# All q and k transposed by PE, the whole residual by transposing transfers, single PSUM banks and a new list: retention followed by a gated MLP

## Chip, core and metric

The kernel runs on one core of a Trainium2 chip. The core has five engines that run on their own queues: PE (TensorE, matmuls, with its weight loads shown apart as PEld), DVE (VectorE), ACT (ScalarE), POOL (GpSimd) and SP (SyncE, which here only issues transfers). They meet through semaphores. [...] Sixteen DMA engines carry the transfers. The metric is the device time of one execution in microseconds (us), lower is better.

## What is computed

Eight sequences of 576 positions, eight heads of 64. The first part is a retention layer: scores without softmax, each multiplied by a power of the head's decay, and zero for keys behind the query. The second is a gated MLP whose gate mixes positions with a 576 x 576 matrix.

```python
scores = scale * np.matmul(q, k.transpose(0, 1, 3, 2))
Dmat = np.where(rel >= 0, gamma[:, None, None] ** rel[None, :, :], 0.0)
x = heads_side_by_side(np.matmul(scores * Dmat, v))      # (8, 576, 512)
h = gelu_tanh(x @ w_in)                                  # (8, 576, 1024)
u, v = h[..., :512], h[..., 512:]
v_n = (v - mean(v)) / np.sqrt(var(v) + 1e-06) * g_ln
v_s = np.einsum('ts,bsd->btd', w_sg, v_n) + b_sg[None, :, None]
out = x + (u * v_s) @ w_out
```

## The kernel before

**Tiling.** Two sequences make a pair p (0 to 3): 1152 positions, nine tiles of 128. Tile 4 holds the end of one sequence and the start of the other. Each pair is cut into five blocks (`RB`): four of 256 positions and, in the middle, one of 128. Blocks are numbered b = 0 to 19. The decay is split into a power for the query and one for the key or value, so that only the block's own part needs a mask (0 or 1), and what lies before a block comes from a running state.

**Steps of a block.** `a_load` loads q, k, v (lines 324 and 327; q of two neighbouring blocks at once, tile `ldq`, except in the joint blocks 0, 1 and the middle ones, which keep q and k in one tile and are transposed together). `a_prep` (lines 340 to 370) multiplies q and v by the powers and casts k to bf16, mostly on POOL. Then q and k are transposed so that the head's dimension lies on partitions: by PE in `a_T` (line 407: 32 matmuls with an identity for a unit of 2048 columns) and a copy from PSUM on DVE, `a_Tev` (line 422), or by one transposing transfer, `a_TX` (line 427). Two limits, `TBQ` and `TBK`, both 10, say up to which block PE does it: pairs 0 and 1 by PE, and in pairs 2 and 3 all but the joint blocks by transfers. `a_S` (line 458) computes the scores of two heads' pairs at a time, `a_Sev` (lines 471, 474) multiplies them by the mask on DVE. `a_Z` (line 494) computes k^T v, `a_Zsum` and `a_Zev` (lines 519 to 528) keep the running state in fp32 and a bf16 copy. `a_O` and `a_O2` (line 540) sum the block's own part and the state's part, `a_Oev` (line 597) moves the result to the tile `xT` on ACT.

**Steps of the MLP.** For each tile i: `m_V` (line 608), gelu on ACT (`m_Vg`, line 615), mean and variance on DVE (`m_stats`, lines 623 and 624), the factor on POOL (`m_rs`, lines 628 to 631), normalizing on ACT (`m_norm`, lines 640 and 643). `m_U` (line 655) and `m_Ug` (line 665) give u in transposed form. `m_W` (line 674) mixes the positions of a sequence with the transposed w_sg (`wT`, built by PE at line 792), `m_Wg` (line 684) multiplies by u on DVE. `m_O` (line 705) multiplies by w_out. The residual x is added in one of two ways: for pairs below `XP` (= 1, so pair 0) by four identity matmuls into the same PSUM tile (line 700) and a plain copy on ACT (line 722), for the others by a transposing transfer `m_X` (line 716) and an add on DVE (line 724). `m_store` (line 729) stores 128 rows.

**PSUM.** Two pools: `psP` has two tiles of two banks each (transposes, scores, outputs of a block), `psD` four tiles of one bank (all else). A tile that is asked for waits until the reader of the tile that held its place is done.

**Order.** All steps are jobs with a number, and `ORDER` (lines 20 to 54) is a list of job numbers written out: it is the order in which the steps are issued, and so the order of each engine's queue. `f2w128` and the like are filler matmuls on a tile of zeros (line 225). `3@267` holds job 3, a load on SP's queue, until PE has done job 267; eleven transfers are held so. The planner class emits the list and does not reorder it. The durations and due times given to `add` are not used when the kernel is built.

Of the kernel before, what the change touches and what calls it, by code (L numbers as in the profile page):

```python
# [61 lines left out]
class Job:  # L62
    def __init__(self, eng, dur, due, fn, deps=(), new=None, uses=(), mode=None, nbytes=0, run=0, what="", behind=None, since=0.0, lag=0.0, ins=0, port=False, parts=1):
# [12 lines left out]
class Planner:  # L76
# [27 lines left out]
def kernel(  # L104
# [46 lines left out]
    XP = 1  # L151
    TBQ, TBK = 10, 10
# [65 lines left out]
    def fill(spec):  # L218
# [3 lines left out]
        def f():  # L222
            scr = psD.tile([128, 512], F32, name="scr", tag="d")
# [18 lines left out]
    def win_load(half):  # L242
# [22 lines left out]
    def sg_load():  # L265
# [821 lines left out]
```

## Time and profile before

| what | us |
|---|---|
| time, median of 3 runs | 209.55 |
| lowest and highest run | 209.48, 209.73 |
| span of the profiled execution, first to last instruction | 207.8 |
| ACT busy, evictions of x (line 597) | 20.8 |
| ACT busy, normalizing (line 643) | 25.2 |
| DVE busy, gate products (line 684) | 27.6 |
| DVE busy, statistics (line 623) | 24.6 |
| POOL waiting for DVE's statistics (line 628) | 36.5 |

The profile is one execution, of which only the span is given: the time that the runs measure includes what lies before the first and behind the last instruction. Busy time counts an engine's instructions as the profiler recorded them. The ends of matmuls are modelled, so for a row of them the distance from one start to the next tells what they cost. In a line of the groups, `DVE COPY qT<-pp 128x2048 bf16<-128x2048 bf16 x5 | 6.1, 1214 | 2.1` reads: five copies, 6.1 us together, 1214 ns each, and 2.1 us of idle time on the engine just before them. An arrow in brackets names what ended that idle time.

### The profile page before, as it was taken

How to read it: one execution, taken by the hardware profiler on the slowest of the kernel's cores; microseconds unless marked ns; L12 is line 12 of the kernel's file. 1: busy time of each engine (PE TensorE's matmuls, PEld its weight loads, DVE VectorE, ACT ScalarE, POOL GpSimd, SP SyncE). 2: the span in 40 equal slices, each digit the busy share in tenths (PEclk: the TensorE clock that was granted, in tenths of full speed). 3: DMA queues.
4: the chain of work that ended last, by engine and by line, in shares of the span. 5: the costliest groups of instructions: out<-in, count | busy, mean ns of one | idle time of the engine just before them, and what ended most of it. 6: DMA issues, size and time to landing. Idle time of an engine off the chain costs nothing. (4 is left out here: it accounts for less than half of the span.)

```text
span 207.8 us, 7603 instructions
## 1 busy us (share of the span) xinstructions
PE 189.1 (91%) x3231; PEld 130.0 (63%) x3260; DVE 146.6 (71%) x287; ACT 116.3 (56%) x207; POOL 118.3 (57%) x169
## 2 busy tenths in 40 slices
PE   3277989999999979999999999999999999999992
PEld 3256467786667655666777676676675776556651
DVE  3767549897597669646968479669695648876672
ACT  5263398864659436689477565745827580536300
POOL 8747348864858799884659628760558813022000
PEclk9999999999999999999999999999999999999998
DMA  5999989989958999599999989999899999659765
GB/s 163 287 313 215 312 282 317 295 241 326 304 123 226 264 335 336 161 231 174 221 288 351 179 183 333 250 139 206 232 299 334 182 242 253 171 169 169 261 140 203
DMA packets 93844, 50.45 MB, mean 243 GB/s; under 512 B 44970, under 2 KB 87218, under 8 KB 93810
## 3 DMA queue, kind: packets, MB, share of 16 engines
q1 hardware_dynamic: 93792, 49.96, 93.8%
q8 instruction: 25, 0.41, 0.9%
q14 instruction: 9, 0.07, 0.1%
q10 hardware_dynamic: 18, 0.00, 0.0%
HBM read 32.79 MB, written 9.44 MB: 203 GB/s over the span
## 5 line engine op out<-in xcount | busy, mean ns | idle before, releaser
L471 DVE TENSOR_TENSOR ret<-pp,msk 128x1024 bf16<-128x1024 f32 x32 | 38.3, 1214 | 7.5 <-PE pp L458 7.4
L674 PE MATMUL wp<-wT,vn 128*128 128x288 bf16 x256 | 40.6, 286 | 0.0
L370 POOL TENSOR_TENSOR vb<-ld,gpow 128x1024 bf16<-128x1024 f32 (+1 forms) x20 | 34.5, 1731 | 10.2 <-PE pp L458 6.1
L608 PE MATMUL hv<-w_in,xT 128*128 128x512 bf16 x132 | 36.5, 393 | 1.9 <-ACT xT L597 1.0
L684 DVE TENSOR_TENSOR uT<-wp,uT 128x288 bf16<-128x288 f32 x64 | 27.6, 450 | 14.9 <-PE wp L674 10.3
L655 PE MATMUL hu<-xT,w_in 128*128 128x256 bf16 (+1 forms) x320 | 36.3, 262 | 0.0
L615 ACT ACTIVATE vg<-hv 128x512 f32<-128x512 f32 x36 | 21.2, 595 | 25.0 <-PE hv L608 20.7
L705 PE MATMUL op<-w_out,uT 128*128 128x512 bf16 (+1 forms) x131 | 33.5, 373 | 0.8 <-issue 0.2
L655 PEld LDWEIGHTS <-w_in 128*128 128x128 bf16 x320 | 28.1, 98 | 6.2
L623 DVE BATCH_NORM_STATS2 bst<-vg 128x6 f32<-128x512 f32 x36 | 24.6, 683 | 8.8 <-ACT vg L615 8.7
L597 ACT ACTIVATE xT<-pp 128x512 bf16<-128x512 f32 (+1 forms) x40 | 20.8, 549 | 17.2 <-PE pp L540 17.2
L370 POOL TENSOR_TENSOR qb<-ldq,gpow 128x1024 bf16<-128x1024 f32 x14 | 26.4, 1902 | 5.3 <-DMA ldq<-in_q_dram 5.3
L674 PEld LDWEIGHTS <-vn 128*128 128x128 bf16 x256 | 24.3, 98 | 8.2
L643 ACT ACTIVATE vn<-vg,mv 128x512 bf16<-128x512 f32 x32 | 25.2, 809 | 6.5 <-POOL mv L631 6.4
L628 POOL TENSOR_SCALAR mv<-mv 128x2 f32<-128x2 f32 (+1 forms) x20 | 4.5, 224 | 41.6 <-DVE mv L624 36.5
L665 ACT ACTIVATE uT<-hu 128x512 bf16<-128x512 f32 x36 | 20.7, 594 | 10.2 <-PE hu L655 10.1
L724 DVE TENSOR_TENSOR ob<-op,xr 128x512 f32<-128x512 f32 (+1 forms) x28 | 18.4, 669 | 5.8 <-PE op L705 5.5
L608 PEld LDWEIGHTS <-xT 128*128 128x128 bf16 x144 | 13.4, 100 | 14.2 <-ACT xT L597 1.6
L705 PEld LDWEIGHTS <-uT 128*128 128x128 bf16 x148 | 13.5, 98 | 11.4
L674 PE MATMUL wp<-wT,vmid 128*128 128x288 bf16 x64 | 18.2, 287 | 0.1
L360 POOL CAST kb<-ld 128x1024 bf16<-128x1024 f32 x14 | 14.5, 1037 | 4.8 <-DMA ld<-in_k_dram 4.8
L629 POOL TENSOR_TENSOR mv<-mv,mhalf 128x2 f32<-128x2 f32 (+1 forms) x20 | 14.1, 705 | 1.7
(100 smaller groups left out, 238.2 us busy)
## 6 DMA issues: line engine op xcount, KB each, us to landing
out_dram<-ob SPq DMA_DIRECT2D x35, 256.0 KB, 3.1
ld<-in_v_dram SPq DMA_DIRECT2D x16, 512.0 KB, 5.7
ld<-in_k_dram SPq DMA_DIRECT2D x16, 512.0 KB, 6.5
ldq<-in_q_dram SPq DMA_DIRECT2D x7, 1024.0 KB, 10.4
xT<-in_moe_w_sg_dram SPq DMA_DIRECT2D x2, 576.0 KB
ld<-in_q_dram SPq DMA_DIRECT2D x2, 512.0 KB, 5.2
xT<-in_moe_w_in_dram SPq DMA_DIRECT2D x1, 1024.0 KB
ld<-in_q_dram SPq DMA_DIRECT2D x8, 128.0 KB, 4.2
```

Source lines behind the costliest of these rows:

```text
L370: ve.tensor_tensor(dst, src, g.unsqueeze(len(src.shape) - 1).to_broadcast(list(src.shape)), op=Alu.mult)
L471: ins = nc.vector.tensor_tensor(ret[:].rearrange("p r (k t) -> p (r k) t", k=2), sc[:].rearrange("p r (k t) -> p (r k) t", k=2), (msk2 if ...
L597: nc.scalar.activation(dst, src, Act.Copy)
L608: ins = nc.tensor.matmul(hv[:], xTs[p][:, m, kk, :], w_in[:, kk, F2:], start=(kk == 0), stop=(kk == KK - 1))
L615: unfence(nc.scalar.activation(vgs[i][:], cur.pop(("hv", i))[:], Act.Gelu_apprx_tanh), ("V", i))
L623: nc.vector.bn_stats(bst[:], vgs[i][:])
L643: nc.scalar.activation(vn[:], vg[:], Act.Identity, scale=mv[:, s, 2:3], bias=mv[:, s, 3:4])
L655: ins = nc.tensor.matmul(hu[:, n, :], w_in[:, kk, 128 * c:128 * c + 128], xTs[p][:, m:m + w, kk, :], start=(kk == 0), stop=(kk == KK - 1), ...
L665: unfence(nc.scalar.activation(uTs[p][:, c0:c1, 128 * m:128 * m + 128 * w], cur.pop(("hu", i, half))[:], Act.Gelu_apprx_tanh), ("U", i, half))
L674: ins = nc.tensor.matmul(ps[:], vns[t0 + j][e][:, 128 * c:128 * c + 128], wT[e][j][:, half * HS:(half + 1) * HS], start=(j == 0), stop=(j ...
L684: ins = nc.vector.tensor_tensor(uTs[p][:, c, col:col + HS], cur.pop(("wp", b, c, half))[:], uTs[p][:, c, col:col + HS], op=Alu.mult)
L705: ins = nc.tensor.matmul(op[:], uTs[p][:, c, r], w_out[:, c, cs], start=(p >= XP and c == 0), stop=(c == KK - 1), skip_group_check=True)
```

## The change

Both limits on PE's transposes go from 10 to 20, and `XP` from 1 to 0. The two PSUM pools become one of eight single banks, so a transposed unit, a score tile and a block's output are two tiles of one bank each instead of one of two; their readers become two instructions each for transposes (`a_Tev`) and scores (`a_Sev`). A helper `copy` picks the engine, many jobs have a second engine (`alt`), and a number with `~` in the list is run on it. 55 entries of the new list carry that mark: by it, 18 evictions of x and three of the state go from ACT to DVE, 13 half copies of transposes, three of wT and three of the running state from DVE to ACT, eight casts of k from POOL to ACT, v of block 0 and q and v of block 1 from POOL to DVE, q and k of block 0 to POOL, and one cast of each half of w_in changes its engine. The list is new for all engines. It has no fillers and no held transfers.

```diff
     BUFS = dict(ld=8, ldq=2, qb=2, kb=2, vb=3, qT=2, kT=2, ret=4, zb=6, run=4, xT=2, uT=2, vg=3, mv=3, vn=11, ob=4,
-                xr=3, pp=2, d=4)
+                xr=3, d=8)
...
-    psP = ctx.enter_context(tc.tile_pool(name="psP", bufs=2, space=bass.MemoryType.PSUM))
-    psD = ctx.enter_context(tc.tile_pool(name="psD", bufs=4, space=bass.MemoryType.PSUM))
+    ps = ctx.enter_context(tc.tile_pool(name="ps", bufs=8, space=bass.MemoryType.PSUM))
+
+    def copy(eng, dst, src):
+        if eng == "ACT":
+            return nc.scalar.activation(dst, src, Act.Copy)
+        return (nc.vector if eng == "DVE" else nc.gpsimd).tensor_copy(dst, src)
...
-    XP = 1
-    TBQ, TBK = 10, 10
+    XP = 0
+    TBQ, TBK = 20, 20
...
-        tp = psP.tile([128, 2, 1024], BF, name="pp", tag="pp")
+        tp = [ps.tile([128, 1024], BF, name="tp", tag="d") for r in range(2)]
...
-    def a_Tev(b, t):
-        dst, w = new_T(b, t)
-        ins = nc.vector.tensor_copy(dst[:, :w].rearrange("p (c w) -> p c w", c=2), st.pop((b, "tp", t))[:, :, :w // 2])
+    def a_Tev(b, t, r, eng):
+        if ("Tw", b, t) not in cur:
+            cur["Tw", b, t] = new_T(b, t)
+        dst, w = cur["Tw", b, t]
+        ins = copy(eng, dst[:, r * w // 2:(r + 1) * w // 2], st.pop((b, "tp", t, r))[:, :w // 2])
...
-        sc = psP.tile([128, 2, 512], F32, name="pp", tag="pp")
+        sc = [ps.tile([128, 512], F32, name="sc", tag="d") for r in range(2)]
...
-    def a_Sev(b, g):
+    def a_Sev(b, g, r):
...
+            m = (msk2 if joint(b) else msk4)[:].rearrange("p a b t -> p (a b t)").unsqueeze(1).to_broadcast([128, 2, 256])
+            ins = nc.vector.tensor_tensor(ret.rearrange("p (k t) -> p k t", k=2), sc[:].rearrange("p (k t) -> p k t", k=2), m, op=Alu.mult)
...
-        ot = psP.tile([128, 2, 512], F32, name="pp", tag="pp")
+        ot = [ps.tile([128, 512], F32, name="ot", tag="d") for c in range(2)]
...
-        nc.scalar.activation(dst, src, Act.Copy)
+        copy(eng, dst, src)
```

The beginning of the two lists, by steps. SP before: q0, v0, k0, k1, the tail of w_sg, q1, v1, first half of w_in (held), q2, k2, v2, the rest of w_sg, q3, second half of w_in (held). SP after: q0, k0, q2, v1, k1, v0, the tail of w_sg, first half of w_in, q1, v2, second half of w_in, a part of w_sg, k2, the rest of w_sg, v3, q3. PE before: fillers, Z0, transposes and scores of block 0, block 1, V0, V1, block 2, fillers, V4, wT. PE after: block 0 (transposes, scores, Z, O), block 1's transposes, Z and scores, V0, V1, the first U, block 2 and O of block 1, wT, V2, V3, V4.

More of the change, by code (lines that the diff above doesn't have):

```diff
@@ L62, with __init__ @@
 class Job:
-    def __init__(self, eng, dur, due, fn, deps=(), new=None, uses=(), mode=None, nbytes=0, run=0, what="", behind=None, since=0.0, lag=0.0, ins=0, port=False, parts=1):
+    def __init__(self, eng, dur, due, fn, deps=(), new=None, uses=(), mode=None, nbytes=0, run=0, what="", behind=None, since=0.0, lag=0.0, ins=0, port=False, parts=1, alt=None, after=()):
+        self.alt, self.after = alt, [d for d in after if d is not None]
         self.what, self.behind, self.since, self.lag, self.ins, self.port, self.parts = what, behind, since, lag, ins, port, parts
@@ L284, in sg_load @@
         ld.append(add("SP", 450.0, 0.0, f_last, new=b1, nbytes=64 * S * 4, run=2304))
-        return ld, [add("ACT", 677.0, 0.0, lambda j=j: g(j), deps=[ld[j // 2]], uses=[bA if j < 4 else b1]) for j in range(SB)]
+        return ld, [add("ACT", 677.0, 0.0, lambda eng="ACT", j=j: g(j, eng), deps=[ld[j // 2]], uses=[bA if j < 4 else b1]) for j in range(SB)]
     def wo_load():
@@ L292, in wo_load, with g @@
         ld = add("SP", 550.0, 0.0, f, deps=[jw[0, 0], jw[0, 1]], uses=[bB], nbytes=1 << 20, run=2048)
-        def g(c):
-            nc.scalar.mul(w_out[:, c, :], wst["in", 0][:, c, :DM], col[:, c:c + 1])
-        return [ld], [add("ACT", 714.0, 0.0, lambda c=c: g(c), deps=[ld], uses=[bB]) for c in range(KK)]
+        def g(c, eng):
+            if eng == "ACT":
+                nc.scalar.mul(w_out[:, c, :], wst["in", 0][:, c, :DM], col[:, c:c + 1])
+            else:
+                nc.vector.tensor_scalar(w_out[:, c, :], wst["in", 0][:, c, :DM], col[:, c:c + 1], None, op0=Alu.mult)
+        return [ld], [add("ACT", 714.0, 0.0, lambda eng="ACT", c=c: g(c, eng), deps=[ld], uses=[bB]) for c in range(KK)]
     st = {}
@@ L387, in fence, with read @@
             tc.declare_fence(ins.ins, group=fenced[what])
+    def read(ins, what, n):
+        cur["left", what] = cur.get(("left", what), n) - 1
+        unfence(ins, what, cur["left", what] == 0)
     def unfence(ins, what, last=True):
@@ L394, in a_T @@
     def a_T(b, t):
-        tp = psP.tile([128, 2, 1024], BF, name="pp", tag="pp")
-        st[b, "tp", t] = tp
+        tp = [ps.tile([128, 1024], BF, name="tp", tag="d") for r in range(2)]
+        for r in range(2):
+            st[b, "tp", t, r] = tp[r]
         ns = RB[b % NBK][0]
@@ L447, in a_S @@
         cs = 64 * ns
[L448 to L449 removed]
+        sc = [ps.tile([128, 512], F32, name="sc", tag="d") for r in range(2)]
+        for r in range(2):
+            st[b, "sc", g, r] = sc[r]
         st[b, "ret", g] = new("ret", [128, 2, 512], BF)
@@ L853 @@
                      deps=sg + [j_z0], new=bf, mode="F", ins=11)
-            jt[e, j] = add("DVE", 450.0, jb.due + 500.0, lambda e=e, j=j: evac_wT(e, j), deps=[jb], uses=[bf])
+            jt[e, j] = add("DVE", 450.0, jb.due + 500.0, lambda eng="DVE", e=e, j=j: evac_wT(e, j, eng), deps=[jb], uses=[bf], alt=("ACT", 660.0))
     for b in range(NBL):
@@ L875 @@
         kfst = not jn and half_of(b) == 0
-        jk = add(eng, 855.0 * h + 183, t0 - 4000.0, lambda b=b, eng=eng: a_prep(b, "k", None, eng),
-                 deps=[J["ld", b, "k"]] + (jqs if jn and b else [J["k", b - 1]] if not jn and not kfst else []), behind=jqs[0] if jn else None,
+        jk = add(eng, 855.0 * h + 183, t0 - 4000.0, lambda eng=eng, b=b: a_prep(b, "k", None, eng), alt=("POOL" if eng == "ACT" else "ACT", 855.0 * h + 183),
+                 deps=[J["ld", b, "k"]], after=jqs if jn else [J["k", b - 1]] if not kfst else [],
                  new=B_qkb["k", U_] if kfst else None,
                  uses=[B_ld[b, "k"]] + ([B_qkb["q", U_]] if jn else [] if kfst else [B_qkb["k", U_]]))
-        jvv = add("POOL", 1715.0 * h + 190, t0 - 2000.0, lambda b=b: a_prep(b, "v"), deps=[J["ld", b, "v"]],
+        jvv = add("POOL", 1715.0 * h + 190, t0 - 2000.0, lambda eng="POOL", b=b: a_prep(b, "v", None, eng), alt=("DVE", 126.0 + 1100.0 * h) if b < 3 else None, deps=[J["ld", b, "v"]],
                   new=B_vb[b], uses=[B_ld[b, "v"]])
@@ L890 @@
             if b < (TBQ if t == "q" else TBK) or jn:
-                tpb = Buf("pp")
-                jT = add("PE", 565.0 * w, t0, lambda b=bb, t=t: a_T(b, t), deps=pre, new=[tpb], uses=[B_qkb[x]], mode="T", ins=int(66 * w))
-                jTe = add("DVE", 160 + 1060.0 * w, t0 + 700.0, lambda b=bb, t=t: a_Tev(b, t), deps=[jT], new=[B_qkT[x]], uses=[tpb])
-            else:
-                jTe = add("SP", 4800.0 * w, t0, lambda b=bb, t=t: a_TX(b, t), deps=pre, new=[B_qkT[x]], uses=[B_qkb[x]],
-                          nbytes=524288 * w, run=256)
+                tpb = [Buf("d"), Buf("d")]
+                jT = add("PE", 469.0 if w == 1 else 238.0, t0, lambda b=bb, t=t: a_T(b, t), deps=pre, new=tpb, uses=[B_qkb[x]], mode="T", ins=int(66 * w))
+                jTe = []
+                for r in range(2):
+                    jTe.append(add("DVE", 84 + 597.0 * w, t0 + 700.0, lambda eng="DVE", b=bb, t=t, r=r: a_Tev(b, t, r, eng), deps=[jT], after=jTe,
+                                   new=[] if r else [B_qkT[x]], uses=[tpb[r]] + ([B_qkT[x]] if r else []), alt=("ACT", 160 + 860.0 * w)))
+            else:
+                jTe = [add("SP", 4800.0 * w, t0, lambda b=bb, t=t: a_TX(b, t), deps=pre, new=[B_qkT[x]], uses=[B_qkb[x]],
+                           nbytes=524288 * w, run=256)]
             J["T" + t, U_] = jTe
@@ L911 @@
             jS = add("PE", 205.0 if ns == 2 else 120.0, t0 + PR["S"] + PR["S2"] * g, lambda b=b, g=g: a_S(b, g), deps=tdeps,
-                     new=[scb, B_ret[b, g]], uses=B_T, mode="Q", ins=33)
-            J["Se", b, g] = add("DVE", 1220.0 if ns == 2 else 690.0, jS.due + 500.0, lambda b=b, g=g: a_Sev(b, g),
-                                deps=[jS], uses=[scb, B_ret[b, g]])
+                     new=scb + [B_ret[b, g]], uses=B_T, mode="Q", ins=33)
+            for r in range(2):
+                J["Se", b, g, r] = add("DVE", 691.0 if ns == 2 else 425.0, jS.due + 500.0, lambda b=b, g=g, r=r: a_Sev(b, g, r),
+                                       deps=[jS], uses=[scb[r], B_ret[b, g]])
     B_run = {}
@@ L929 @@
                 B_run[b, c] = Buf("run")
-            J["run", b, c] = add("DVE", 400.0, due, lambda b=b, c=c: a_Zsum(b, c), deps=[jz] + ([J[("run",) + was]] if was else []),
+            J["run", b, c] = add("DVE", 400.0, due, lambda eng="DVE", b=b, c=c: a_Zsum(b, c, eng), alt=("ACT", 400.0) if fst else None, deps=[jz] + ([J[("run",) + was]] if was else []),
                                      new=B_zb[b, c] if fin else B_run[b, c], uses=[zpb[c]] + ([B_run[was]] if was else []))
@@ L934 @@
             else:
-                J["zb", b, c] = add("ACT", 380.0, due + 100.0, lambda b=b, c=c: a_Zev(b, c), deps=[jz] if fst else [J["run", b, c]],
+                J["zb", b, c] = add("ACT", 380.0, due + 100.0, lambda eng="ACT", b=b, c=c: a_Zev(b, c, eng), alt=("DVE", 400.0) if fst else None, deps=[jz] if fst else [J["run", b, c]],
                                     new=B_zb[b, c], uses=[zpb[c]] if fst else [B_run[b, c]])
@@ L939 @@
             zs = ((b - 1, 1), (b, 0))
-        otb = Buf("pp")
+        otb = [Buf("d"), Buf("d")]
         own = 580.0 if ns == 2 else 215.0
         st[b, "zs"] = zs
-        deps = [J["v", b]] + J["tdeps", b] + [J["Se", b, g] for g in range(ns)] + [J[("zb",) + z] for z in zs if z]
+        deps = [J["v", b]] + J["tdeps", b] + [J["Se", b, g, r] for g in range(ns) for r in range(2)] + [J[("zb",) + z] for z in zs if z]
         uses = [B_vb[b], J["B_T", b][0]] + [B_ret[b, g] for g in range(ns)] + [B_zb[z] for z in zs if z]
-        jO1 = add("PE", own, t0 + PR["O"], lambda b=b: a_O(b), deps=deps, new=[otb], uses=uses, mode="Q", what=("O", b), ins=33 * ns + 16)
-        jO = add("PE", 112.0, jO1.due + 300.0, lambda b=b: a_O2(b), deps=[jO1], lag=270.0, uses=uses + [otb], mode="Q", what=("O2", b), ins=18)
+        jO1 = add("PE", own, t0 + PR["O"], lambda b=b: a_O(b), deps=deps, new=otb, uses=uses, mode="Q", what=("O", b), ins=33 * ns + 16)
+        jO = add("PE", 112.0, jO1.due + 300.0, lambda b=b: a_O2(b), deps=[jO1], lag=270.0, uses=uses + otb, mode="Q", what=("O2", b), ins=18)
         if n == 0:
@@ L950 @@
             fst = n == 0 and c == 0
-            J["x", b, c] = add("ACT", 600.0 if ns == 2 else 385.0, jO.due + 700.0 + 100 * c, lambda b=b, c=c: a_Oev(b, c),
-                               deps=[jO] + ([J["x", p * NBK, 0]] if not fst else []), new=B_x if fst else None,
-                               uses=[otb] + ([] if fst else [B_x]))
+            J["x", b, c] = add("ACT", 600.0 if ns == 2 else 385.0, jO.due + 700.0 + 100 * c, lambda eng="ACT", b=b, c=c: a_Oev(b, c, eng), alt=("DVE", 681.0 if ns == 2 else 416.0),
+                               deps=[jO], after=[J["x", p * NBK, 0]] if not fst else [], new=B_x if fst else None,
+                               uses=[otb[c]] + ([] if fst else [B_x]))
         B_mv = Buf("mv")
@@ L1044 @@
                                        uses=[B_x, B_u], mode="F", ins=17)
-                            jOe = add("ACT", 597.0, due + 700.0, lambda a=a: m_Oev(*a), deps=[jOut], uses=[db, obb])
+                            jOe = add("ACT", 597.0, due + 700.0, lambda eng="ACT", a=a: m_Oev(*a, eng), alt=("DVE", 640.0), deps=[jOut], uses=[db, obb])
                         else:
```

108 lines of the change are left out of this document (52 added, 56 removed), and 68 rows, old and new, of the table ORDER.

## The prediction

> **What bounds the kernel now.** I read the page's busy totals first, then its 40 slices, then the chain that ended last, and then the windows by stage.
>
> ```profile
> PE 189.1 (91%) x3231; PEld 130.0 (63%) x3260; DVE 146.6 (71%) x287; ACT 116.3 (56%) x207; POOL 118.3 (57%) x169
> PE   3277989999999979999999999999999999999992
> DMA  5999989989958999599999989999899999659765
> PE 34%; issue 1%; DVE 0%; DVEq 0%
> 30.00:50.00 20.00, 19.38 (x415) 15.11 (x413) 17.29 (x32) 15.57 (x27) 14.05 (x16) 1.00 1.03 300
> 50.00:80.00 30.00, 28.04 (x572) 19.59 (x576) 21.23 (x39) 16.61 (x32) 23.86 (x26) 1.00 0.98 261
> 80.00:130.00 50.00, 49.40 (x922) 33.77 (x928) 36.45 (x65) 34.24 (x65) 34.39 (x47) 1.00 0.98 242
> 130.00:170.00 40.00, 39.47 (x591) 26.91 (x598) 28.54 (x59) 24.26 (x44) 23.13 (x32) 1.00 1.02 233
> 170.00:200.00 30.00, 29.64 (x342) 18.82 (x346) 21.68 (x40) 10.35 (x19) 4.63 (x9) 1.00 0.84 208
> 200.00:207.80 7.80, 3.73 (x22) 1.97 (x21) 3.55 (x7) 0.00 (x0) 0.00 (x0) 0.92 0.45 169
> ```
>
> In a window row the columns after the length are the busy times of PE, weight loads, DVE, ACT and POOL. From 30 to 200 us PE is busy 165.9 of 170 us: it is the bound, and only 4.1 us of gaps are left there. The chain that ended last is PE alone. The DMA engines are nearly full too (slice digits of 9 almost throughout), but they end almost no wait of PE. So the time is the start (about 30 us, PE slice digits 2 to 9), plus PE's work, plus its gaps, plus a tail of 4.4 us. The change has to be judged by what it does to each of these four.
>
> **PE's work.** Each of the four pairs of sequences has two units whose q and k are transposed apart from the joint ones. Pairs 2 and 3 had these eight transposes (two units, q and k, two pairs) as transposing transfers; now PE does them. In return the residual of pair 0 leaves PE: nine output tiles lose four identity matmuls each.
>
> ```profile
> 38.68 0.64 PE L407 MATMUL pp<-ident,kb 64*128 64x64 bf16 x32
> 39.25 1.05 PE L655 MATMUL hu<-xT,w_in 128*128 128x256 bf16 x8
> 55.61 0.64 PE L407 MATMUL pp<-ident,kb 64*128 64x64 bf16 x32
> 56.09 0.63 PE L407 MATMUL pp<-ident,qb 64*128 64x64 bf16 x32
> 58.39 0.39 PE L700 MATMUL op<-ident,xT 128*128 128x128 bf16 x4
> 58.61 1.03 PE L705 MATMUL op<-w_out,uT 128*128 128x512 bf16 x4
> ```
>
> Ends are modelled, so I take start to start: 32 transposes occupy PE from 38.68 to 39.25 (0.57 us), or from 55.61 to 56.09 (0.48). I take 0.55: eight add **+4.4 us** (ends 3.8 and 4.6). Four identity matmuls take 0.22: nine save **-2.0 us**. Net +2.4 us (1.8 to 2.6). PE being the bound, nothing hides it.
>
> [...]
>
> **The start.** The new list has no filler matmuls, and another order of loads: q0, k0, q2, v1, k1, v0, the tail of w_sg, then the first half of w_in (v first was second), and its steps of the first blocks stand on other engines: v of block 0 and q and v of block 1 are scaled by DVE, q of block 0 by POOL.
>
> ```profile
> 0.00:5.00 5.00, 1.97 (x8) 1.78 (x8) 1.60 (x15) 2.71 (x3) 4.13 (x24) 1.00 0.56 158
> 5.00:10.00 5.00, 1.09 (x25) 0.74 (x29) 3.84 (x15) 1.47 (x3) 4.19 (x7) 1.00 1.20 293
> 10.00:15.00 5.00, 3.67 (x102) 2.89 (x92) 3.01 (x5) 3.46 (x6) 1.94 (x2) 1.00 1.16 296
> ld<-in_v_dram SPq DMA_DIRECT2D x16, 512.0 KB, 5.7
> 7.65 1.90 POOL L370 TENSOR_TENSOR vb<-ld,gpow 128x1024 bf16<-128x1024 f32 x1
> 8.63 1.06 ACT L358 ACTIVATE qb<-ld 128x1024 bf16<-128x1024 f32 x1 [3.20 <-DMA ld<-in_k_dram]
> 20.71 0.61 PE L608 MATMUL hv<-w_in,xT 128*128 128x512 bf16 x1 [0.77 <-ACT xT L597]
> 23.64 1.89 PE L608 MATMUL hv<-w_in,xT 128*128 128x512 bf16 x4
> 27.77 1.60 PE L225 MATMUL scr<-warm 128*128 128x128 f32 x12
> 31.41 0.31 PE L494 MATMUL zp<-vb,qb 64*64 64x64 bf16 x8
> 31.66 1.11 PE L792 MATMUL wtp<-ident,wnat 128*128 128x128 bf16 x15
> 32.69 1.89 PE L608 MATMUL hv<-w_in,xT 128*128 128x512 bf16 x8
> 134.62 0.68 PE pp L540 x40
> 140.39 0.87 PE hu L655 x8
> 149.20 0.86 PE hv L608 x4
> ```
>
> The last column of a window is GB/s: 0.79 MB have come by 5 us and 2.26 MB by 10 us. Three blocks of 512 KB (0.52 MB) make 1.57 MB, by that count at 7.7; the third one's reader starts at 8.63, one us later. Now v0 ends at 2.9 MB: 12.1 by the count, about 13 with that lag, against 7.65 before. Scaling (1.2 on DVE), Z0, the masks of block 0, O0 follow; x0.0, which V0 needs, stands in DVE's queue behind the scaling of q1 and v1, two transposed halves and a cast of w_in's second half, whose data is the 5.9th MB (22 to 23.5 us). So V0 starts near 25 instead of 20.71. From there V0, V1 and the first U run without a break, and I get the last of block 2's Z at about 32, against 31.41. By that point of the list PE has done one U more (0.87), but not V4, three groups of wT (15 matmuls, 31.66 to 32.69) and O of block 2 (half of a full block's 0.68 and some): 0.86 + 1.03 + 0.4 - 0.87, 1.4 us less. With Z2's end (31.66 before) at 32 the shift is +1.7 by this walk; the fillers' 1.8 us of queue time (27.77 to 29.6) may come back in part. I take **+1.0 us**, with -3 (V0 as early as before, and the U early as well) and +4 (w_in or w_sg late by one more block) as ends.
>
> The gate itself: four matmuls of 512 columns took 1.89 at 23.64 and eight of them took 1.89 at 32.69, so PE's pace doubled in between, though the granted clock reads 1.00 throughout. [...]
>
> **The gaps between 30 and 200.** Two things pull apart. The largest gap was one late scaling of q, itself behind a late load:
>
> ```profile
> 76.77 0.64 PE L407 MATMUL pp<-ident,qb 64*128 64x64 bf16 x32 [1.54 <-POOL qb L370]
> POOL qb L370 <- DMA ldq<-in_q_dram: 5.3, 3, 3.1
> L471 DVE TENSOR_TENSOR ret<-pp,msk 128x1024 bf16<-128x1024 f32 x32 | 38.3, 1214 | 7.5 <-PE pp L458 7.4
> L474 DVE TENSOR_TENSOR ret<-pp,msk 128x512 bf16<-128x512 f32 x4 | 2.8, 692 | 2.5 <-PE pp L458 2.4
> L422 DVE COPY qT<-pp 128x2048 bf16<-128x2048 bf16 x5 | 6.1, 1214 | 2.1 <-PE pp L407 2.1
> L422 DVE COPY qT<-pp 128x1024 bf16<-128x1024 bf16 x4 | 2.7, 681 | 0.0
> L724 DVE TENSOR_TENSOR ob<-op,xr 128x512 f32<-128x512 f32 x26 | 17.7, 688 | 5.8 <-PE op L705 5.5
> L597 ACT ACTIVATE xT<-pp 128x512 bf16<-128x512 f32 x32 | 18.0, 592 | 16.7 <-PE pp L540 16.7
> L519 DVE COPY run<-zp 128x256 f32<-128x256 f32 x8 | 3.3, 414 | 0.7 <-PE zp L494 0.7
> ```
>
> Fewer bytes go through transposing transfers (eight of 0.52 MB out, nine tiles of 0.13 MB in), and POOL gives eight casts of k to ACT and three scalings to DVE, and gets one of each for block 0: this 1.5 us should go. SP's queue gets the pair 0 residual transfers between loads, each waiting for its x: a load behind one waits too, but loads run far ahead of their readers.
>
> DVE gets much more, in us of duration. Masks in halves: 64 x 0.692 + 8 x 0.41 against 32 x 1.214 + 4 x 0.692, **+6.0**. Copies of transposes: 32 halves x 0.681 + 8 x 0.41, against 8 x 1.214 + 4 x 0.681, +12.6; the list sends 13 of the halves to ACT, -8.3. Residual adds of nine tiles, +6.2. Eighteen evictions of x move from ACT to DVE (12 full at 0.681, 6 half at 0.41), +10.7. The rest about +1. Together +28: DVE goes from 146.6 to about 173 us. Counted along the list, the 100 us of PE work after the first 10 carry 108 us of DVE durations, where before they carried 85. Durations overlap at their edges (rows summing to 156 make 146.6 busy, 0.94), so DVE must be busy 101 of some 102 us of PE. In the windows to 130 it was busy 75 of 100. What slack there is comes from eight banks in turn, each released by its own eviction, where a double bank waited for one long one. I put the cost of an almost full DVE at +0.5 (0 to +7). The tail keeps its form. Gaps in all: **-1.0**.
>
> **Sum.** 2.4 + 1.0 - 1.0 = +2.4 on the span of 207.8: 210.2. The runs' median (209.55) stands 1.75 above the profiled span, so **212.0 us**.
>
> **Rivals.** 1) *DVE becomes the bound in the middle third.* An in-order engine at 99% of PE's work there waits now and then for an input, and PE then waits for a bank or a mask: at 94% of its pace the 102 us become 108.5. That is +6 in place of the +0.5: 217. For it: the count of 108. Against it: before, at 86% (17.29 of 20), PE lost only 0.6 in 20. It decides when DVE's idle time there exceeds 3%. 2) *The new list packs better than the old* (the other side): the start is 3 us shorter since loads are issued without holds and PE has a U in the start, and PE's gaps fall from 4.1 to 1.1. Then 2.4 - 3 - 3 = -3.6: 206.0. For it: one pool of eight banks takes away the split of two double and four single ones, and DMA is eased. Against it: V0 later by 4 us in my walk. It decides when V0 starts before about 21. 3) *They cancel*: half of these savings against +2.4, 209.6. 4) The change doesn't do what it says: the pool could still pair banks and the eight transposes stay where they were; the diff sets both limits to all 20 blocks and allocates single tiles, so I give this nothing.
>
> **How the numbers follow.** Forecast, 210.0 to 214, 0.40; rival 1, 214 to 219, 0.17; rival 2, 204.5 to 209.1, 0.34; rival 3, 0.09. A measurement can tell about 0.2% (0.4 us) from no change. So faster 0.34, same 0.09, slower 0.57. The range takes in the forecast, rival 3, most of rival 2 and half of rival 1: 205.5 to 217. The likeliest case's own range is 210.0 to 214.
>
> **What would show it.** PE work: 576 matmuls on the line of the transposes instead of 320, none on the identity line L700's. [...] Middle: DVE busy above 9 of 10 between 35 and 130, and PE idle with DVE as releaser if rival 1 holds; PE's busy share over 98% if rival 2 does. POOL's waits for q loads should shrink. I am wrong if V0 starts by 21, or if PE has more than 6 us of gaps after 32.

## The result, and the profile after

The changed kernel took **220.83 us** (median of 4 runs, 219.54 to 222.40), the kernel before, run beside it, 209.64: 1.0529 times as long, with a 95% interval of 1.0480 to 1.0579. The sign of the forecast (212.0) was right, its size was not: 11.2 us more instead of 2.4, and outside the stated range (205.5 to 217). The profiled execution spans 218.6 us (its run took 220.66), 10.8 more than the one before.

From the page of the changed kernel: busy totals, the slices of PE, of PE's clock and of the DMA engines, the first line of the chain that ended last, and the DMA queue for instructions.

```profile
PE 190.4 (87%) x3456; PEld 128.9 (59%) x3456; DVE 166.3 (76%) x364; ACT 122.4 (56%) x203; POOL 109.0 (50%) x160
PE   0426699999699999999999998699999999999992
PEclk9999999999969999999999999999999999999999
DMA  6999999999999997999998999229273915928365
PE 79%; DMA 8%; issue 4%; SPq 2%; DVE 2%; ACT 2%; POOL 1%; DVEq 0%; POOLq 0%; ACTq 0%
q8 instruction: 27, 0.44, 0.9%
```

PE has hardly more to do (190.4 against 189.1); it is the span that grew. Two marks are new: a slice of the clock at 6 tenths, about a quarter of the way, and "issue" in the chain, 4%, time in which PE waited for nothing that the profile shows. The DMA engines are full for the first 25 slices (137 us) and half idle afterwards. The windows of the changed kernel, and the first 30 us of the one before:

```profile
0.00:30.00 30.00, 13.49 (x253) 8.67 (x254) 18.25 (x52) 13.95 (x21) 14.19 (x36) 1.00 1.06 279
30.00:50.00 20.00, 19.08 (x461) 14.30 (x460) 17.10 (x38) 16.73 (x29) 14.98 (x19) 1.00 1.08 268
50.00:80.00 30.00, 27.12 (x598) 17.58 (x599) 23.78 (x54) 19.58 (x34) 19.83 (x24) 0.94 1.17 255
80.00:130.00 50.00, 49.13 (x1022) 34.09 (x1024) 44.27 (x91) 32.26 (x57) 35.53 (x39) 1.00 1.09 257
130.00:170.00 40.00, 37.18 (x684) 25.25 (x674) 31.76 (x71) 20.86 (x34) 20.38 (x32) 1.00 0.58 144
170.00:200.00 30.00, 30.00 (x379) 19.94 (x370) 21.38 (x45) 15.84 (x28) 3.33 (x10) 1.00 0.66 151
200.00:218.60 18.60, 14.36 (x96) 9.09 (x93) 9.78 (x19) 3.17 (x5) 0.74 (x3) 1.00 0.52 158
```

```profile
0.00:30.00 30.00, 19.40 (x379) 13.79 (x382) 17.90 (x48) 15.31 (x26) 18.25 (x43) 1.00 0.95 256
```

PE's idle time is 16.5 us before 30 (before: 10.6), 7.5 from 30 to 200 (before: 4.1), and 4.2 behind it (before: 4.1): 9.5 us more, and 1.3 of busy time make the 10.8. The split is not exact: the kernel before has 3231 records of matmuls for 3260 weight loads, and a matmul without a record can show as idle time. What PE waited for after 30, from the waits of the changed kernel (total, times, longest):

```profile
PE ot L552 <- issue: 2.8, 3, 2.2
PE sc L471 <- issue: 2.5, 1, 2.5
PE hu L672 <- issue: 0.5, 1, 0.5
PE tp L417 <- issue: 0.5, 1, 0.5
PE op L722 <- ACT xT L148: 0.4, 1, 0.4
PE tp L417 <- ACT zb L148: 0.3, 1, 0.3
```

6.3 us without a releaser; in the kernel before it was 0.4. All waits in the list make 7.0 us, in the kernel before 2.4 of its 4.1. In the timeline these waits stand inside jobs:

```profile
57.84 0.30 PE L552 MATMUL ot<-qT,zb 64*64 64x128 bf16 x6
60.36 0.24 PE L552 MATMUL ot<-qT,zb 64*64 64x128 bf16 x2 [2.22 <-issue]
61.65 1.70 PE L620 MATMUL hv<-w_in,xT 128*128 128x512 bf16 x4
65.37 1.03 PE L620 MATMUL hv<-w_in,xT 128*128 128x512 bf16 x4
135.78 0.30 PE L471 MATMUL sc<-qT 64*64 64x64 bf16 x12
138.58 0.22 PE L471 MATMUL sc<-qT 64*64 64x64 bf16 x4 [2.50 <-issue]
```

PE stops after 6 of 8 matmuls, and after 12 of 16, of a job that reads tiles and banks which its first matmuls had already used: missing data are an unlikely reason. What is missing is the instructions. The trace has 27 transfers of 16 KB on the instruction queue, and 27 times 256 is 6912, the number of PE's matmuls and weight loads. Of the runs below, one with 256 PE instructions more (128 weight loads and 128 matmuls) has one transfer more, and one with 672 fewer has three less:

```profile
q8 instruction: 28, 0.46, 0.9%
q8 instruction: 24, 0.39, 0.8%
```

Numbered, the five longer stops lie 256 instructions, or a multiple of 256, apart. So one transfer is a block of 256 instructions of PE, and each of these stops is at the end of a block. From the trace's record of those transfers, in the time of the rows above:

```
block before it   transfer     transfer   PE goes on   PE stood
begun by PE at    starts at    ends at    at (row)     still (row)
      40.0           43.9        45.0       46.33        0.42
      46.3           51.3        52.5       53.89        0.51
      53.9           57.9        58.9       60.36        2.22
      96.7           98.4        99.6      101.00        0.50
     132.1          135.9       137.1      138.58        2.50
```

In these traces a block was fetched about when PE began the one before it, not sooner: with half idle DMA engines, from 148 us on, the transfers started between 2.0 us before and 1.8 us after that moment. With full DMA engines they started later, 3.9 to 5.0 us after it in the first three rows and 2.6 on the mean of the 14 blocks begun from 46 to 130 us (in the kernel before, whose engines were nearly as full, 1.3; why its transfers waited less was not shown). In the five rows PE went on 1.4 to 1.5 us after the transfer ended, and in none of the runs did it begin a block less than 1.2 us after. A block with 41 matmuls of the MLP among its 128 lasted 7.9 us (from 101.0); two with 17 and 14, the rest transposes, scores, Z and O, were used up in 4.2 and 4.0 (from 53.9 and 132.1), and at their ends PE stood still for 2.22 and 2.50 us. In the kernel before the transfers from 40 to 130 ended 1.9 us or more before they were needed.

The first long stop has a second price: the four matmuls of 512 columns at 61.65 took 1.70, those at 65.37 took 1.03. The clock record reads half from 61.9 to 65.3. From 61.65 to 65.37 PE did 0.86 of V, twice 0.36 of scores and 0.62 of W at the full pace (the rows at 60.67 to 61.65): 2.2 us of work in 3.7, so **1.5 us lost**.

The start went as the walk had it:

```profile
26.07 3.60 PE L620 MATMUL hv<-w_in,xT 128*128 128x512 bf16 x8 [0.28 <-DVE xT L149]
29.46 1.86 PE L672 MATMUL hu<-xT,w_in 128*128 128x256 bf16 x8
32.73 0.29 PE L506 MATMUL zp<-vb,qb 64*64 64x64 bf16 x8
```

V0 at 26.07 (forecast 25), Z2 at 32.73 (forecast about 32), against 31.41 before and with 1.4 us less work done: 2.7 us by the same account. The balance of the 10.8: PE's work 2.2 (64 transposes take 1.04 here), start 2.7, gaps 3.4, half pace 1.5, tail 0.2; 0.8 is left over. Counted by the waits listed, the gaps are 4.6 instead of 3.4, so the balance is good to about a microsecond.

### The profile page after: what moved, and what is told of

It is laid out like the page before. It is cut to its first block, busy times and chain, and to the rows that moved or that the text cites. A ratio compares the mean times of both kernels' runs of the same rounds, so it can differ in the third digit from the quotient of the medians.

```text
span 218.6 us, 8070 instructions
## 1 busy us (share of the span) xinstructions
PE 190.4 (87%) x3456; PEld 128.9 (59%) x3456; DVE 166.3 (76%) x364; ACT 122.4 (56%) x203; POOL 109.0 (50%) x160
## 4 chain that ended last, share of the span: by engine, by line
PE 79%; DMA 8%; issue 4%; SPq 2%; DVE 2%; ACT 2%; POOL 1%; DVEq 0%; POOLq 0%; ACTq 0%
PE wp L691 19%; PE hv L620 15%; PE hu L672 14%; PE op L722 14%; PE ot L552 6%; DMA uT<-in_moe_w_in_dram 4%; PE tp L417 4%; PE sc L471 4%; PE zp L506 2%; DMA ld<-in_q_dram 2%; DMA ld<-in_v_dram 2%; SPq L335 1%; PE wtp L809 1%; SPq L332 1%; DVE ob L741 0%
## 5 line engine op out<-in xcount | busy, mean ns | idle before, releaser
L485 DVE TENSOR_TENSOR ret<-sc,msk 128x512 bf16<-128x512 f32 x64 | 41.5, 679 | 5.8 <-PE sc L471 5.7
L691 PE MATMUL wp<-wT,vn 128*128 128x288 bf16 x256 | 41.3, 289 | 0.0
L620 PE MATMUL hv<-w_in,xT 128*128 128x512 bf16 x144 | 38.6, 399 | 0.3 <-DVE xT L149 0.3
L375 POOL TENSOR_TENSOR vb<-ld,gpow 128x1024 bf16<-128x1024 f32 (+1 forms) x18 | 31.8, 1770 | 12.9 <-DMA ld<-in_v_dram 11.5
L672 PE MATMUL hu<-xT,w_in 128*128 128x256 bf16 (+1 forms) x320 | 37.3, 266 | 0.5 <-issue 0.5
L722 PE MATMUL op<-w_out,uT 128*128 128x512 bf16 (+1 forms) x148 | 35.4, 374 | 0.4 <-ACT xT L148 0.4
L701 DVE TENSOR_TENSOR uT<-wp,uT 128x288 bf16<-128x288 f32 x64 | 26.9, 448 | 5.5 <-PE wp L691 2.6
L741 DVE TENSOR_TENSOR ob<-op,xr 128x512 f32<-128x512 f32 (+1 forms) x37 | 24.3, 671 | 8.2 <-PE op L722 7.9
L552 PE MATMUL ot<-qT,zb 64*64 64x128 bf16 (+1 forms) x256 | 12.4, 224 | 3.3 <-issue 2.8
L148 ACT ACTIVATE xT<-ot 128x512 bf16<-128x512 f32 (+1 forms) x22 | 12.0, 577 | 5.5 <-PE ot L552 5.5
L641 POOL TENSOR_TENSOR mv<-mv,mhalf 128x2 f32<-128x2 f32 (+1 forms) x20 | 13.7, 687 | 1.7
```

The lines of the kernel that those rows point to most:

```text
L375: ve.tensor_tensor(dst, src, g.unsqueeze(len(src.shape) - 1).to_broadcast(list(src.shape)), op=Alu.mult)
L485: ins = nc.vector.tensor_tensor(ret.rearrange("p (k t) -> p k t", k=2), sc[:].rearrange("p (k t) -> p k t", k=2), m, op=Alu.mult)
L552: nc.tensor.matmul(ot[bank][64 * c:64 * c + 64, j * cs:(j + 1) * cs], lhsT, rhs, start=(bank, c) not in begun, stop=True, skip_group_check ...
L620: ins = nc.tensor.matmul(hv[:], xTs[p][:, m, kk, :], w_in[:, kk, F2:], start=(kk == 0), stop=(kk == KK - 1))
L672: ins = nc.tensor.matmul(hu[:, n, :], w_in[:, kk, 128 * c:128 * c + 128], xTs[p][:, m:m + w, kk, :], start=(kk == 0), stop=(kk == KK - 1), ...
L691: ins = nc.tensor.matmul(wp[:], vns[t0 + j][e][:, 128 * c:128 * c + 128], wT[e][j][:, half * HS:(half + 1) * HS], start=(j == 0), stop=(j ...
```

## The experiments

**Theory A**: PE runs out of instructions where small matmuls come fast and the DMA engines are full. **Theory B**: PE's time is work and waits for data alone; an unmarked wait is only an unmarked releaser. Other rivals: the almost full DVE, the clock at the start, the late start itself, loads.

**1. More instructions in the kernel before.** The same stretch of PE time, once in 256 instructions and once in 22:

```diff
-217 447 449 403 46 410
+217 447 449 f128w64 403 46 410
...
+            def small():
+                scr = [psD.tile([128, 1024], BF, name="scr", tag="d") for r in range(2)]
+                for i in range(n):
+                    r, o = i % 2, 64 * (i // 2 % 16)
+                    R = slice(64 * r, 64 * r + 64)
+                    nc.tensor.transpose(scr[r][:, o:o + 64], ident[R, :], ident[R, R])
```

> The kernel before, with 128 transposes of 64 x 64 on an idle pair of banks put into PE's queue ahead of the first W of pair 1 (about 66 us): 256 more PE instructions (weight load and matmul each), all in one place. By the rows of transposes in this case (64 in 1.04 us) they are 2.1 us of PE work. Theory A (PE's instructions come in blocks of 256 through the DMA engines, and a block eaten in 2 us cannot be replaced in that time while the DMA engines are full): PE stands still without a releaser behind them, 1.5 to 3.5 us, and the clock may close for 3.4 us after that: 4 to 7 us over before, 213.5 to 217. Theory B (PE's time is the work of its instructions and waits for data alone): 2.1 us, 212.

```diff
-217 447 449 403 46 410
+217 447 449 f11w512 403 46 410
...
+            def large():
+                scr = psD.tile([128, 512], F32, name="scr", tag="d")
+                for _ in range(n):
+                    nc.tensor.matmul(scr[:], w_in[:, 0, :128], w_in[:, 0, :512], start=True, stop=True, skip_group_check=True)
```

> The control to the run with 128 small transposes: the kernel before, with 11 matmuls of 512 columns at the same place, 22 instructions and, at 0.216 us each, 2.4 us of PE work. Theory A and theory B alike: 2.4 us over before, 212, and no stall without a releaser. If it costs as much as the 128 transposes, it is the place in the list that costs, not the number of instructions.

Measured: 215.53 us with the small ones, 1.0282 (1.0233 to 1.0332); 210.85 with the large ones, 1.0052 (1.0013 to 1.0090). The timeline with the 128 small transposes:

```profile
66.84 1.75 PE L227 MATMUL scr<-ident 64*128 64x64 bf16 x107
71.97 0.48 PE L227 MATMUL scr<-ident 64*128 64x64 bf16 x21 [3.39 <-issue]
72.38 0.42 PE L688 MATMUL wp<-wT,vmid 128*128 128x288 bf16 x1
72.59 1.17 PE L688 MATMUL wp<-wT,vn 128*128 128x288 bf16 x4
76.00 0.65 PE L688 MATMUL wp<-wT,vn 128*128 128x288 bf16 x4
```

and with the 11 large matmuls:

```profile
66.44 2.55 PE L233 MATMUL scr<-w_in 128*128 128x512 bf16 x11
68.82 0.29 PE L688 MATMUL wp<-wT,vmid 128*128 128x288 bf16 x1
68.94 0.65 PE L688 MATMUL wp<-wT,vn 128*128 128x288 bf16 x4
```

The small ones stop after 107 of 128, for 3.39 us, in the midst of a job that waits for nothing. The transfer of the next block ran from 69.3 to 70.5, and PE went on 1.5 us later. Then W runs at half pace (1.17 against 0.65) for over 3 us. The large ones have neither. Theory A gives the difference of the two times (4.7 us) within 0.4: 3.4 and some 1.7 at half pace. Theory B gives none. That 2.4 us of extra work cost only 1.1 shows that PE's time there was not all on the path: PE's wait of 1.54 us for q is gone in that run.

**2. The same where the DMA engines are half idle.**

```diff
-798 923 925 880 856 875
+798 923 925 f128w64 880 856 875
```

> The changed kernel, with the same 128 small transposes put into PE's queue near 190 us, where the DMA engines are busy half of the time. If it is the number of PE instructions alone that starves PE, there is a stall of 1.5 us or more without a releaser behind them, as in the kernel before at 68.6 to 72. If it is their number while the DMA engines are full (in this part of the changed kernel the next block of instructions was on its way at the latest 0.5 us after the last boundary, against 3.9 to 5.8 us from 40 to 60), there is no stall over 0.5 us, and they cost their own 2.1 us: 2 us over the changed kernel, run beside it.

> The changed kernel as it is, beside the run with the late transposes: 220.8.

Measured: 224.40 and 220.08 us, 1.0682 (1.0578 to 1.0786) and 1.0547 (1.0508 to 1.0586) of the kernel before. The times are too scattered to tell 2 us from 4; the timeline isn't:

```profile
192.80 2.04 PE L235 MATMUL scr<-ident 64*128 64x64 bf16 x128
194.78 0.66 PE L699 MATMUL wp<-wT,vn 128*128 128x288 bf16 x4
```

All 128 in one row, no stop, although, counted by the weight loads, they fill one block almost from its first instruction to its last and use it up in 2.0 us. With the 5.7 us that passed in the run above from a block's begin (66.3) to PE's use of the next (71.97), that would have meant a stop of 3.7. Here the next block had landed at 192.8, 2.0 us before PE needed it. In these two runs it took both: many instructions in little time, and full DMA engines.

**3. Less traffic in the changed kernel**, with all its instructions:

```diff
-            nc.sync.dma_start(f_[:], src[2 * p + e, :, r0:r0 + 128 * s_, :].rearrange("h (p s) d -> p h (s d)", s=s_))
+            hs = slice(0, H // 2) if t != "v" and b > 2 else slice(0, H)
+            nc.sync.dma_start(f_[:, hs], src[2 * p + e, hs, r0:r0 + 128 * s_, :].rearrange("h (p s) d -> p h (s d)", s=s_))
...
+            if ns == 2 and b > 2:
+                src = src[:, :1].to_broadcast(list(src.shape))
```

> The changed kernel with q and k of blocks 3 to 19 (without the middle ones) loaded for four of the eight heads only, and these used twice: some 7 MB of 33 are not read, instructions and their order are the same. Theory A: the fetches of PE's instructions wait less behind data, so the long gaps inside jobs shrink; 3 to 7 us less. Theory B: the loads are not what DVE waits for; 0 to 2 us less. A third: that the instruction queue is slow by itself, whatever the traffic; the gaps stay at 6 us in all.

Measured: 215.37 us, 1.0305 (1.0218 to 1.0393): 5.5 us below the changed kernel. For the four blocks begun from 46 to 63 us the transfers of instructions started 0.8 to 3.2 us after PE's begin of the block before (1.9 to 5.0 for the same four in the changed kernel), and on the mean of those begun from 46 to 130 us 1.7 after, instead of 2.6. The longest stop was 1.0 us, and the clock stayed full:

```profile
PE ot L557 <- issue: 1.5, 3, 0.8
PE sc L476 <- issue: 0.6, 1, 0.6
PE hu L677 <- DVE mv L641: 1.0, 1, 1.0
```

The wait of 1.0 names DVE, but it too is at a block's end: the transfer ended at 84.6 and PE went on at 86.10. The run can't tell the instructions from the loads of data, which have less to wait for as well.

**4. Fewer instructions in the changed kernel.**

```diff
+        lean = not joint(b) and ns == 2
+        if lean:
+            for h in range(4):
+                for r in range(2):
+                    src = parts[(h + r) % len(parts)][0].rearrange("p k s c d -> p (k s c d)")
+                    ins = nc.tensor.transpose(tp[r][:, 128 * h:128 * h + 128], src[:, 128 * (h + 4 * r):128 * (h + 4 * r) + 128], ident[:])
```

> The changed kernel, with the 32 transposes of 64 x 64 of each full q or k unit (sixteen units) replaced by 8 of 128 x 128 into half of the two banks, which the copies read twice: 768 fewer PE instructions (three blocks of 256), while PE's time for a unit goes from about 0.52 to 0.43 (8 x 0.053), -1.4 us in all. The transposed q and k of these units are then not those of the reference. Theory A (instructions run out): the stalls without a releaser, 6.2 us, go for the most part and with them the 3.4 us at half clock: 212 to 215. Theory B (work and data waits alone): 219.4.

Measured: 216.87 us, 1.0345 (1.0293 to 1.0398): 4.0 below the changed kernel, somewhat above the 212 to 215 that theory A had. Fourteen units changed, not the sixteen expected (3120 matmuls instead of 3456), so 672 instructions are gone. Its waits after 26 us:

```profile
PE tp L415 <- POOL kb L149: 2.5, 2, 1.8
PE zp L519 <- POOL vb L375: 1.1, 1, 1.1
PE op L735 <- ACT xT L148: 1.1, 1, 1.1
PE ot L565 <- issue: 0.2, 1, 0.2
```

The stops for instructions are gone (0.2), the clock stays full, but PE now meets POOL's scalings, and those wait for loads: POOL's waits for loads of v from 26 us on are 1.7 us in the kernel before, 9.0 in the changed one and 11.9 here. PE's gaps from 30 to 200 are 7.0 us, hardly fewer than the changed kernel's 7.5. So the price of the stops isn't got back as a whole: with the instructions there, **the data are late**. That both are late for the same reason, the full DMA engines, is likely but not shown by this run. Of the 3.3 us that the span lost, 3.0 are PE's busy time (187.4 instead of 190.4): the half pace (1.5) and PE's own work (some 1.0: a unit's 8 transposes take 0.45 us, its 32 took 0.52). The rest was not traced further.

**5. Both reliefs at once** (the two edits above together).

> The changed kernel with both reliefs at once: q and k of most blocks loaded for four of the eight heads and used twice, and full units transposed by 8 instead of 32 instructions, copied twice from half banks. q and k are thus not those of the reference. Theory A alone (only instructions were short): as the run with fewer transposes, 215 to 217, since its other gaps belong to the list. Theory A with loads (both supplies come over the same full DMA engines, and relieving one lays the other bare): PE's gaps from 30 to 200 fall from 7 us to some 2, 211 to 212.5. What is left above the kernel before is then PE's own work and the start.

Measured: 215.22 us, 1.0242 (1.0160 to 1.0323), four runs from 213.75 to 216.51: no better than less traffic alone (215.37). The 211 to 212.5 of two supplies that only have to be eased together did not come; the number is that of the other case. PE's waits for POOL are gone from its list, so the data did come sooner. The profiled execution, the slowest of the four, still has a stop:

```profile
84.59 1.07 PE L690 MATMUL hu<-xT,w_in 128*128 128x128 bf16 x16
88.07 1.20 PE L690 MATMUL hu<-xT,w_in 128*128 128x256 bf16 x8 [2.42 <-ACT vmid L666]
```

It names ACT, but a block of instructions landed at 86.7 and PE went on 1.4 us later, as in the five rows above (1.4 to 1.5); half pace follows (16 matmuls of scores take 0.64 at 89.20, 0.42 at 80.48). In the run with an earlier start as well (below), the stop at the same place names nothing:

```profile
87.03 1.75 PE L690 MATMUL hu<-xT,w_in 128*128 128x256 bf16 x8 [2.19 <-issue]
```

The two runs with the granted clock at 1.00 took 213.75 and 214.27. What is left above the kernel before even there, some 4 us, is of the size of PE's own work and the start, but what it consists of was not shown.

**6. The start.** Two versions of the list start V0 sooner:

```diff
-114 115 10 338~ 354 356 232
+114 115 338~ 354 356 10 232
```

> The changed kernel, with one entry of the list moved: the DVE cast of one half of w_in's second half (it ended a wait of 1.59 us for its transfer at 24.72, ahead of the eviction of x that V0 waited for) goes behind that eviction and the running sums of block 1. V0 then should start near 23.9 instead of 26.07. If the start is on the path with its full length, 2 us less: 218.7. If the first U or w_in's arrival takes it back, or PE runs out of instructions at other places, nothing: 220.8.

```diff
-112 111~ 82 353 23 81 113 114 115 10 338~ 354 356 232 229 340 24 31 339 343
+112 111~ 353 23 113 114 115 338~ 354 356 10 232 229 340 24 31 339 82 81 343
```

> The changed kernel with three entries of its list moved: the late cast as in the run before (DVE), and ACT's two placings of constants (four and two copies, 4 us of ACT from 20.6 to 24.6) behind the second eviction of block 0's x, for which the scores of block 1 wait for a bank, and V0 with them. V0 should start near 24 instead of 26.07. If the start is on the path: 2 us less, 218.8. If the supply of instructions and loads sets the pace behind it, the 2 us come back as waits of PE between 40 and 110: 220.8.

> The run with both reliefs (half of the loads of q and k, fewer transposes), with the list of the run with the earlier start: the late cast of w_in and the placing of constants behind the eviction of x. q and k are again not those of the reference. In the run with the start alone, block 2's Z ended 1.1 us sooner and nothing was gained. If it was the supply of loads and instructions that took this back, it shows here: 1 to 1.5 us below the run with both reliefs, 213.5 to 214. If the list itself takes it back: 215.

Measured: 222.11 us (1.0581, 1.0496 to 1.0666) with the late cast, 223.17 (1.0619, 1.0541 to 1.0697) with the constants moved too, and 215.23 (1.0309, 1.0227 to 1.0392) with both reliefs as well. In the second:

```profile
25.13 0.61 PE L620 MATMUL hv<-w_in,xT 128*128 128x512 bf16 x1
31.60 0.29 PE L506 MATMUL zp<-vb,qb 64*64 64x64 bf16 x8
```

Z2 came 1.1 us sooner than in the changed kernel, and nothing was won, with the supplies eased or not: PE busy from 30 to 50 fell from 19.08 to 17.77 us. So the 2.7 us of the account are lost there, but one of them given back is no gain. What a start as short as the one before would be worth stays open.

**7. The rivals in the list.** Evictions of x back on ACT (18 marks taken out, as the first of these):

```diff
-114 115 10 338~ 354 356
+114 115 10 338 354 356
```

> The changed kernel with the 18 evictions of x that were given to DVE back on ACT, in the same places of the list: 10.7 us of DVE's work less, 10 of ACT's more. Theory A: the gaps inside PE's jobs stay, time within 2 us of 220.8. Theory B: DVE is relieved where it was fullest, 4 to 6 us less, 215 to 217.

222.83 us, 1.0637 (1.0516 to 1.0758), with DVE at 158.9 us busy instead of 166.3: no gain. ACT had 7.7 us more to do (130.1), which may have cost something; but it speaks against DVE as the bound, as do the waits of the changed kernel after 30 us, which name DVE nowhere.

Fillers as in the kernel before, behind Z0 and block 1's scores:

```diff
-9 105~ 331 333~ 5 4~
+9 105~ 331 f4w128 333~ 5 4~
...
-354 356 232 229 340 24
+354 356 232 f6w128 229 340 24
```

> The changed kernel with filler matmuls back at two places of the start, behind Z of block 0 and behind the first scores of block 1 (4 and 6 matmuls of 128 columns in fp32). If the late opening of the clock gate costs time (V0, V1 and the first U ran at half pace until 31.3 us), the gate opens by about 26 and 1 to 2.5 us go: 218 to 220. If DVE's queue sets the start (the output of block 1 waits for its last mask at 30.7), nothing goes: 220 to 221.5. Theories A and B on the middle say nothing else here.

223.35 us, 1.0607 (1.0458 to 1.0756): no gain. With them the clock is full sooner (from 29.4 us instead of 31.1), but V0 comes over 2 us later (28.78).

PE's jobs moved by a few places in the list, so that small and large matmuls mix and no block of 256 is eaten in under 4 us:

```diff
-237 85 359 361 377 91 92 86~ 362
+237 85 359 377 91 92 86~ 361 362
...
-33 124 379 471 121 351
+33 124 379 99 471 121 351
```

> The changed kernel with the same jobs on the same engines, but PE's jobs moved by at most eight places in the list so that a stretch of 256 PE instructions (one fetch of 16 KB) takes 4 us or more everywhere after the start, where the shortest took 2.0. Theory A (PE runs out of instructions, because blocks of 256 with many small matmuls are eaten before the next block has come through the busy DMA queues): the gaps of 2.2, 2.5 and several of 0.5 us inside a job, which no semaphore ends, go for the most part, and with the longest the 3.4 us at half clock; 6 to 8 us less, near 213. Theory B (DVE, 166 us busy, holds PE back): DVE's work is unchanged, so 219 to 222. Theory C (the start and PE's added work explain all): 220 to 222.

**230.24 us**, 1.1019 (1.0931 to 1.1108), 9.4 us worse than what it was to mend. The stops without a releaser fell from 6.3 to 1.6 us and the clock stayed full, as theory A has it, but other waits came:

```profile
PE op L722 <- DVE uT L701: 2.0, 2, 1.1
PE sc L471 <- ACT kT L148: 1.2, 2, 0.8
PE ot L552 <- issue: 1.1, 2, 0.9
```

Jobs moved for the sake of the instructions stood ahead of their data: PE's gaps from 30 to 200 are 13.7 us. That is 6.2 of the 10.0 us that the span grew; what the rest consists of was not shown. The run gives no price for the stops; it shows how little slack the list has.

**8. An attempt to beat both.** The q that PE waited 1.54 us for in the kernel before, scaled earlier:

```diff
-394 140 145 146 149 143 144 511
+394 140 143 145 146 149 144 511
```

> The kernel before, with one entry moved: POOL scales the first half of q of block 8 (landed long before) ahead of the cast of block 8's k instead of behind it. In its profile POOL was idle for 0.96 us ahead of that cast and 0.85 and 0.67 us ahead of the two steps behind it, each for a load, and PE waited 1.54 us at 76.77 for the second half of the same q. With the first half in those gaps the second half ends near 74.9 and the wait goes: 1.5 us less if PE's gaps are on the path there, 208.1, faster than both kernels; no change if the loads take the time back a few steps later.

```profile
76.43 0.64 PE L407 MATMUL pp<-ident,qb 64*128 64x64 bf16 x32
```

The wait is gone from that row; the time is 209.15 us, 1.0006 (0.9964 to 1.0048): no difference that can be measured. Two waits of 0.7 us, for another scaling and for wT, came instead. The largest wait of PE, taken out by itself, bought nothing.

## Why the prediction was off

- **The gaps are the step that failed**: "Gaps in all: -1.0". They are +3.4, and 1.5 at half pace come with them. The step looked only at waits for data: q's late load, POOL's queue, DVE's fullness. It had the DMA engines as "nearly full too", ending "almost no wait of PE", and didn't ask what else comes over them. More PE instructions were priced by their time alone; that the same change packs them closer, with transposes, scores, Z and O in a row, had no term and no rival. Of the 7.5 us of gaps 6.3 are stops for instructions. The waits for data did shrink, as the step had it: PE's one wait of 1.54 us for q has no counterpart.
- **The start** was walked rightly (25 and 32 against 26.07 and 32.73), and taken at +1.0 where the walk itself said +1.7 and the account now says 2.7. The reason in the walk was half of it: the cast of w_in came last (V0's 0.28 us of wait ends with the DVE step behind it), but with it moved, V0 came at 25.64, 0.4 sooner. ACT's placing of constants held x0.1, whose bank the next scores needed, nearly as long. What the prediction calls the gate, the doubling of PE's pace, came late too: the clock record begins, at full, at 25.6 us in the kernel before and at 31.1 here, and until then V0 and V1 (3.60 us for eight matmuls at 26.07, against 1.89 in the kernel before at 32.69) and U (1.86 at 29.46, against 1.05 there at 39.25) ran at half pace. What sets its time was not shown.
- **PE's work** was right: +2.4 forecast, 2.2 by the rows here. 576 transposes on their line, as said:

```profile
L417 PE MATMUL tp<-ident,qb 64*128 64x64 bf16 x352 | 8.4, 199 | 1.1 <-issue 0.5 <-POOL qb L149 0.4
L417 PE MATMUL tp<-ident,kb 64*128 64x64 bf16 x224 | 4.7, 190 | 0.3 <-ACT zb L148 0.3
```

- **Rival 1** (DVE the bound) fell: DVE is busy 44.27 of 50 us from 80 to 130 (89%), and 85 of 100 from 30 to 130, less than the 99% that the count along the list gave, and 166.3 in all where 173 was forecast. PE's gaps from 80 to 130 are 0.9 us, none of them DVE's. Rivals 2 and 3 fell with the sign. That the sign was right is no luck, since work and start together cost 4.9 of the 10.8; but about half was in no term.
- **POOL's waits for q** shrank as forecast, but those for v grew. "Loads run far ahead of their readers" was too much for either list: from 26 us on POOL waited 12.7 us for loads in the kernel before and 19.0 in the changed one.
- Of the two signs that were to say "I am wrong", one came: more than 6 us of gaps after 32.

## What to carry to other kernels

Count PE's instructions, not only its time: where the list packed many small matmuls into 2 to 4 us per 256 matmuls and weight loads, and the DMA engines were full, PE stood still in the midst of a job (2.22 and 2.50 us in the changed kernel, 3.39 with 128 transposes put in), and the profile shows it as "issue" without a releaser. Look for a stop inside a job first, since a wait for data is an unlikely reason there; a stop between two jobs can carry another engine's name (the 0.99 us at 86.10 with less traffic named DVE). Then ease the traffic there (5.5 us here) or use fewer instructions (4.0 us). Spreading the small matmuls among large ones took the stops away here but gained nothing, since jobs moved ahead of their data. A stop of 2.22 us cost 1.5 more here: behind it the clock read half for 3.4 us.

## What the hardware showed unexpectedly

- PE's instructions came in 16 KB transfers of 256 (27 transfers, 0.44 MB, for 6912 matmuls and weight loads; 128 transposes more with their weight loads, one transfer more), and in no run here did the transfer of a block start more than 2.2 us before PE began the block ahead of it. From 30 us on, waiting for them cost 0.4 us in the kernel before and 6.3 in the changed one.
- From PE's begin of a block to the start of the next one's transfer 3.9 to 5.0 us passed with full DMA engines (blocks begun from 40 to 54 us), 0.8 to 3.2 with less traffic (46 to 63 us), and from 148 us on, with half idle engines, the transfer started 2.0 us before to 1.8 after. A transfer took 0.9 to 1.8 us in the changed kernel (0.9 to 2.0 in the one before), and PE went on 1.2 us or more after its end in all runs (1.4 to 1.5 where it stood waiting in the changed kernel's five rows).
- Behind a stop of 2.22 us the clock read half for 3.41 us (61.9 to 65.3), behind one of 2.50 us in the same execution (138.58) it did not: eight matmuls of 512 columns at 140.22 took 1.89, the full pace. Half pace also followed stops of 3.39 us (128 transposes put in) and of 2.42 and 2.19 (both reliefs, without and with the earlier start). The clock record of the changed kernel has it full for 30.72 us from 31.1 on, half for 3.41 and full for 153.60, which are 9, 1 and 45 times 3.41. Why one stop was followed by half pace and the longer one was not, no run shows.
